# x of batch 0 on partitions 0-47 and 64-111, block 0 read in two parts, its zb made on chip, and one conversion moved to tick 96

## The chip, the core and the metric

The kernel runs on one core of one Trainium2 chip. The core has five engines that run side by side and meet at semaphores: PE (TensorE, the matmuls; its weight loads are shown apart as PEld), DVE (VectorE), ACT (ScalarE), POOL (GpSimd) and SP (SyncE, which here only issues DMAs). DMAs issued by SP, ACT and POOL run on 16 DMA engines. The metric is the device time of one execution in microseconds (us), lower is better. Times are given as medians of several runs; one execution was also profiled, and its trace is what the rows below come from.

## The reference

```python
def reference(x, w_in, w_out, w2_in, w2_out, alpha):   # x: 2 x 3008 x 256, float32
    X = np.fft.fft(np.fft.fft(x, axis=1), axis=2).real     # as float32
    t = X.reshape(6016, 256)
    h = t @ w_in                                           # 256 x 2048
    g = np.where(h > 0, h, np.exp(np.minimum(h, 0)) - 1)   # ELU
    t = g @ w_out                                          # 2048 x 256
    h = t @ w2_in
    g = np.maximum(h, 0) + alpha * np.minimum(h, 0)        # PReLU, alpha per column
    return g @ w2_out
```

The names stand for moe_w_in and so on. The weights arrive as float64; the kernel converts them to float32 on the chip.

## The kernel before

**The Fourier transform.** 3008 = 47 x 64. Stage A (`stage_a`, L146) multiplies x by a 47-point DFT matrix `f47` (L152): x of a batch lies in four chunks `xc` of 96 rows x 8 x 256, and each chunk takes four matmuls of 512 columns, whose results ACT copies to `uc` (L154). `store_u` (L161) writes `uc` to the DRAM tensors `ud`, one for each of three blocks g of the batch, and `load_v` (L168) reads a block back in another layout as `vt` (128 x 8 x 256). Stage B (`stage_b`, L199) multiplies `vt` by a 64-point DFT matrix `r64`, in two halves q = 0 and 1 (L206, L207); ACT rounds each half to float32r as `hi` (L210) and DVE subtracts it to get `lo` (L211). Both stand in `zt`, the input of layer 1. The 256-point transform along the last axis is not done on data: `w_fold` (L261) multiplies it into `w_in` of layer 1.

**zb.** One row of the transform needs a correction of rank one. `delta` (L178) computes 8 x 64 numbers of a block from `vt`, ACT copies them and writes them to DRAM (`nd`), and `load_zb` (L191) reads them back as 512 numbers repeated on 128 partitions. DVE adds `zb` times a number for each row (`an_sb`) to the first product (L420).

**The layers.** There are six blocks of up to 1024 columns (t = 0 and 1, 512 or 482 each) and, for each layer, 16 tiles f of the 2048 inner columns. One pair of block and f is a tick; ticks 0 to 95 are layer 1, 96 to 191 layer 2. A tick runs `gemm1` (L316), the nonlinearity on DVE and ACT, a split of the result `et` into `hi` (ACT, L398) and `lo` (POOL in layer 1, DVE in layer 2, L404), and three ticks later `gemm2` (L330), which adds three products (hi w_hi, hi w_lo, lo w_hi) to each of four accumulators. A product in float32r is one pass; a matmul of stage A, of the fold and of stage B in float32 is two, shown as x2.

**Weights.** `ld` reads a chunk of 512 columns or rows in float64; `conv_y` (ACT, L240) and the three steps of `conv_s` (DVE, L250, L252, L254) make float32 of one half of it; `w_split` makes `hi` (ACT, L293) and `lo` (POOL, L294), or `w_fold` does so for `w_in` of layer 1.

**What sets the order.** All is written out by hand. `START` is the list of what comes before tick 0, in the order in which each engine gets it; an entry names a function and its arguments (`('a', c, i)` is half a chunk of stage A, `('v', g)` a `load_v`, `('conv', kind, c, i)` half a weight chunk). Later work hangs on ticks by tables: `CONV2` has for each chunk of layer 2, counted from tick 80, the tick of its read, of the conversions of its two halves, a 1 or 3 that says whether the three DVE steps stand in three ticks or in one, and the ticks of the two splits. Each engine works through its instructions in program order. SP issues its DMAs in order too, and one that waits holds up those behind it. A pool with the tag `big` has seven buffers for `c256_sb`, `xc`, `uc`, `vt`, `zt` and later tiles; a new tile waits for the readers of the one whose buffer it gets.

```python
for eng, p0, p1 in ((nc.sync, 0, 96),) if b else ((nc.sync, 0, 64), (nc.scalar, 64, 96)):
    eng.dma_start(out=t[p0:p1, i * n:(i + 1) * n], in_=x[b, p0:p1, c * 8 + i * n:c * 8 + (i + 1) * n, :])
```

These two lines of `load_x` (L140, L141) put x of batch 0 on partitions 0 to 95: SP reads 64 rows of each chunk, ACT 32.

Of the kernel before, what the change touches and what calls it, by code (L numbers as in the profile page):

```python
# [11 lines left out]
ALU = mybir.AluOpType
# [14 lines left out]
    ('r64',), ('load', 'i', 1, 0), ('c256',), ('load', 'i', 1, 1), ('load', 'o', 1, 0),  # L27
    ('a', 0, 0), ('a', 0, 1), ('a', 1, 0), ('a', 1, 1), ('a', 2, 0), ('a', 2, 1), ('conv', 'i', 0, 0), ('conv', 'i', 0, 1), ('a', 3, 0),
    ('a', 3, 1), ('v', 0),
    ('conv', 'i', 1, 0), ('conv', 'i', 1, 1), ('fold', 0), ('an', 0), ('conv', 'o', 0, 0), ('fold', 1), ('conv', 'o', 0, 1), ('warm',), ('delta',), ('zb',),  # L30
    ('u', 1), ('split', 'o', 0, 0), ('alpha',), ('load', 'o', 1, 1), ('u', 2), ('v', 1), ('load', 'x', 1, 0),
    ('load', 'i', 1, 2), ('load', 'x', 1, 1), ('load', 'o', 1, 2), ('load', 'x', 1, 2), ('load', 'i', 1, 3), ('load', 'o', 1, 3),
    ('b',), ('an', 1),
# [41 lines left out]
def tile_fft_moe_elu_moe_prelu(  # L75
# [57 lines left out]
    def load_x(b, c, parts=1):  # L133
        if b:
            t = wp.tile([96, 8, 256], F32, tag=("sa", "sb", "sc")[c % 3], name="xc")
        else:
            t = big.tile([96, 8, 256], F32, tag="big", name="xc")
        n = 8 // parts
        for i in range(parts):
            for eng, p0, p1 in ((nc.sync, 0, 96),) if b else ((nc.sync, 0, 64), (nc.scalar, 64, 96)):  # L140
                eng.dma_start(out=t[p0:p1, i * n:(i + 1) * n], in_=x[b, p0:p1, c * 8 + i * n:c * 8 + (i + 1) * n, :])  # L141
# [178 lines left out]
    def gemm2(L, bl, f, first, last, hi, lo):  # L320
# [6 lines left out]
        for t in range(2):  # L327
            for d in range(2):
                for i, (a, b) in enumerate(PASSES):
                    mm(out=accs[L, bl][d][t][:, 0:n], lhsT=w[:, a, o, d * 128:(d + 1) * 128],  # L330
                       rhs=(hi, lo)[b][:, t, 0:n], start=(f == first and i == 0), stop=(f == last and i == 2))
# [153 lines left out]
    with tc.manual_schedule():  # L485
        nc.sync.dma_start(out=f47_sb, in_=f47)
        for c in range(4):
            load_x(0, c, 1 if c else 2)
        warm = wk.tile([128, 2, 512], F32, tag="h", name="warm")
        nc.vector.memset(warm, 0.0)  # L490
        wps = mmtile()
        for i in range(2):
            mm(out=wps, lhsT=warm[:, 0, 0:128], rhs=warm[:, 1, :], start=True, stop=True)
        def warm_up():
            wps = mmtile()
            for i in range(3):
# [143 lines left out]
```

## Time and profile before

| what | value |
|---|---|
| median of 3 runs | 1011.43 us (1008.5 to 1012.55) |
| the profiled execution | 1008.45 us |
| its span, first to last instruction | 1006.7 us |
| PE busy | 987.3 us (98%) |
| DVE busy | 684.8 us (68%) |
| ACT busy | 684.3 us (68%) |
| POOL busy | 310.4 us (31%) |
| mean granted clock of PE | 0.998 |

Engine times are busy times in the span; the engines overlap. A granted clock of 1 is 2.4 GHz, 0.5 is 1.2 GHz. In the rows, a line such as L316 is a line of the kernel before, `out<-in` names the tiles written and read, x3 a count of instructions merged into one row, and a bracket at the end the idle time of that engine just before, with what ended it. PEq, SPq and so on are an engine's sequencer, which issues DMAs; "issue" is time for which the profile shows no wait.

### The profile page before, as it was taken

What the parts mean: (1) busy time and instruction counts of PE and PEld (TensorE: products, weight loads), DVE (VectorE), ACT (ScalarE), POOL (GpSimd) and SP (SyncE); (2) the same over time, 40 slices, a digit from 0 to 9 for tenths busy, and PEclk for the clock granted to TensorE, in tenths of its full rate; (3) what the DMA queues carried; (4) which work ended last, traced back from release to release, by engine and by line L of the source; (5) the groups of instructions that cost most, each with busy time, mean ns of one, the idle gap of its engine ahead of it and who ended that gap; (6) DMA issues with size and microseconds to landing.
All of it is one profiled execution on the core that took longest, in us unless ns stands there. A gap on an engine that the chain in (4) does not pass through costs nothing.

```text
span 1006.7 us, 11887 instructions
## 1 busy us (share of the span) xinstructions
PE 987.3 (98%) x4354; PEld 799.4 (79%) x4354; DVE 684.8 (68%) x908; ACT 684.3 (68%) x991; POOL 310.4 (31%) x232
## 2 busy tenths in 40 slices
PE   8899999999999999999999999999999999999998
PEld 3576767788888888887788888888888888888887
DVE  1787988987887788899878655654544555455444
ACT  4577776766887788778787765655656666666654
POOL 0355667765656666566512100000000000000000
PEclk9999999999999999999999999999999999999999
DMA  9793322000000000124100001010010001001001
GB/s 275 206 320 87 82 74 94 1 12 1 1 11 1 11 1 1 42 86 153 57 1 0 1 1 42 1 43 1 1 39 1 1 1 42 1 1 42 0 1 40
DMA packets 20130, 44.65 MB, mean 44 GB/s; under 512 B 1988, under 2 KB 9412, under 8 KB 18632
## 3 DMA queue, kind: packets, MB, share of 16 engines
q1 hardware_dynamic: 18400, 41.61, 13.3%
q10 hardware_dynamic: 1416, 2.12, 0.7%
q8 instruction: 34, 0.56, 0.2%
q0 software_dynamic: 256, 0.17, 0.1%
q14 instruction: 24, 0.20, 0.1%
HBM read 31.41 MB, written 12.48 MB: 44 GB/s over the span
## 4 chain that ended last, share of the span: by engine, by line
PE 84%; DVE 9%; DMA 2%; issue 2%; ACT 1%; SPq 0%; POOL 0%; DVEq 0%; ACTq 0%
PE acc L330 45%; PE mmt L316 21%; PE eet L316 15%; DMA w<-w_in 2%; DVE ht L422 1%; DVE et L389 1%; DVE pt L420 1%; DVE sg L252 1%; DVE et L386 1%; DVE w L254 1%; PE eet L268 1%; DVE sg L250 1%; PE eet L152 1%; DMA xc<-x 1%; PE mmt L206 1%
## 5 line engine op out<-in xcount | busy, mean ns | idle before, releaser
L330 PE MATMUL acc<-hi,wo 128*128 128x512 f32 (+1 forms) x1536 | 470.5, 388 | 3.9 <-ACT hi L398 2.1
L330 PEld LDWEIGHTS acc<-hi,wo 128*128 128x128 f32 x1536 | 288.7, 188 | 60.8 <-ACT hi L398 2.5
L404 POOL TENSOR_TENSOR lo<-et,hi 128x512 fp32r<-128x512 f32 (+1 forms) x192 | 266.0, 1407 | 143.3 <-ACT hi L398 102.8
L330 PE MATMUL acc<-lo,wo 128*128 128x512 f32 (+1 forms) x768 | 298.6, 389 | 2.7 <-POOL lo L404 2.6
L398 ACT ACTIVATE hi<-et 128x1024 fp32r<-128x1024 f32 (+2 forms) x193 | 199.5, 1034 | 135.6 <-PE acc L330 103.1
L404 DVE TENSOR_TENSOR lo<-et,hi 128x512 fp32r<-128x512 f32 (+1 forms) x192 | 121.9, 676 | 152.3 <-ACT hi L398 152.2
L330 PEld LDWEIGHTS acc<-lo,wo 128*128 128x128 f32 x768 | 145.1, 189 | 33.7 <-POOL lo L404 5.7
L440 ACT ACTIVATE et<-ht 128x1024 f32<-128x1024 f32 (+2 forms) x97 | 100.4, 1035 | 91.4 <-DVE ht L422 86.4
L316 PE MATMUL mmt<-zt,wi 128*128 128x512 f32 (+1 forms) x462 | 122.0, 396 | 2.7 <-ACT zt L210 1.2
L391 DVE SCALAR_TENSOR_TENSOR et<-et,nal_sb,ht 128x1024 f32<-128x1024 f32 (+1 forms) x96 | 121.7, 1268 | 0.0
L316 PE MATMUL eet<-xhi,wi 128*128 128x512 f32 (+1 forms) x384 | 117.4, 387 | 1.4 <-DVE et L386 1.4
L316 PE MATMUL mmt<-xhi,wi 128*128 128x512 f32 (+1 forms) x384 | 117.3, 387 | 0.0
L316 PEld LDWEIGHTS mmt<-zt,wi 128*128 128x128 f32 x462 | 86.4, 188 | 25.6 <-issue 3.0
L316 PEld LDWEIGHTS eet<-xhi,wi 128*128 128x128 f32 x384 | 72.1, 188 | 15.8 <-DVE et L386 1.8
L316 PEld LDWEIGHTS mmt<-xhi,wi 128*128 128x128 f32 x384 | 72.1, 188 | 14.0
L420 DVE SCALAR_TENSOR_TENSOR pt<-zb,an_sb,mmt 128x512 f32<-128x512 f32 (+1 forms) x77 | 56.3, 732 | 30.7 <-PE mmt L316 30.6
L450 ACT ACTIVATE ht<-mmt 128x512 f32<-128x512 f32 (+1 forms) x96 | 56.5, 589 | 26.3 <-PE mmt L316 26.3
L316 PE MATMUL eet<-xlo,wi 128*128 128x512 f32 (+1 forms) x192 | 74.3, 387 | 0.0
L316 PE MATMUL mmt<-xlo,wi 128*128 128x512 f32 (+1 forms) x192 | 74.3, 387 | 0.0
L450 ACT ACTIVATE ht<-eet 128x512 f32<-128x512 f32 (+1 forms) x96 | 56.5, 589 | 22.8 <-PE eet L316 22.8
L389 DVE SCALAR_TENSOR_TENSOR et<-et,ht 128x1024 f32<-128x1024 f32 (+2 forms) x43 | 69.8, 1625 | 0.7 <-ACT et L442 0.7
L386 DVE SCALAR_TENSOR_TENSOR et<-eet,ht 128x512 f32<-128x512 f32 (+1 forms) x108 | 67.8, 668 | 0.0
(83 smaller groups left out, 911.8 us busy)
## 6 DMA issues: line engine op xcount, KB each, us to landing
w<-w_in SPq DMA_DIRECT2D x8, 1024.0 KB, 10.4
w<-w_out SPq DMA_DIRECT2D x8, 1024.0 KB, 11.6
vt<-ud SPq DMA_DIRECT2D x6, 1024.0 KB, 4.8
ud<-uc SPq DMA_DIRECT2D x20, 256.0 KB, 4.2
out_t<-ot SPq DMA_DIRECT2D x16, 256.0 KB, 2.2
xc<-x SPq DMA_DIRECT2D x4, 768.0 KB, 11.3
out_t<-ot SPq DMA_DIRECT2D x8, 241.0 KB, 2.2
xc<-x SPq DMA_DIRECT2D x3, 512.0 KB, 11.4
```

The lines of the kernel that those rows point to most:

```text
L152: mm(out=p[0:96], lhsT=f47_sb, rhs=xc[b, c][:, r0:r0 + 2, :].rearrange("p r j -> p (r j)"), start=True, stop=True)
L206: mm(out=o, lhsT=v[:, k, 0:128], rhs=r64_sb[:, 0:128], start=True, stop=False)
L316: mm(out=p[:, 0:n], lhsT=lhsT, rhs=rhs, start=(i == 0), stop=(i == len(ops) - 1))
L330: mm(out=accs[L, bl][d][t][:, 0:n], lhsT=w[:, a, o, d * 128:(d + 1) * 128], rhs=(hi, lo)[b][:, t, 0:n], start=(f == first and i == 0), sto ...
L386: stt(out=s["e"][:, i, :], in0=s["x"][i], scalar=-1.0, in1=s["h"][:, i, :], op0=ALU.add, op1=ALU.max)
L389: stt(out=s["e"][:, i], in0=s["e"][:, i], scalar=-1.0, in1=s["h"][:, i], op0=ALU.add, op1=ALU.max)
L391: stt(out=s["e"], in0=s["e"], scalar=nal_sb[:, s["f"]:s["f"] + 1], in1=s["h"], op0=ALU.mult, op1=ALU.add)
L398: act(out=s["hi"][:, i, 0:s["n"]], in_=s["e"][:, i], func=ACTF.Copy)
L404: (nc.gpsimd if s["L"] == 1 else nc.vector).tensor_tensor(out=s["lo"][:, i, 0:n], in0=s["e"][:, i, :], in1=s["hi"][:, i, 0:n].bitcast(F32) ...
L420: stt(out=pt[:, 0:n], in0=zb[bl][:, 0:n], scalar=an_sb[:, f:f + 1], in1=p[0], op0=ALU.mult, op1=ALU.add)
L440: act(out=s["e"][:, i], in_=s["h"][:, i], func=ACTF.Relu, scale=-1.0)
L450: act(out=s["h"][:, i, :], in_=p[i], func=ACTF.Relu)
```

## The change

- **x of batch 0** lies on partitions 0 to 47 and 64 to 111. ACT reads the upper 48 rows, SP the lower 48. The rows 32 to 63 of each chunk are first set to zero, by DVE for chunks 0 and 2 and by POOL for 1 and 3; SP's part overlaps them and waits for that, and the matmul takes 112 rows. `f47_ap` is `f47` in the same layout, with zeros between; `f47_sb` is read later, for batch 1. Chunk 0 is cut into 2 and 6 of its 8 groups, instead of 4 and 4.
- **Block 0** is read back as `vt` in two parts: 24 of its 32 rows behind the stores of three chunks, 8 behind the last.
- **zb of block 0** is made on chip. `ready_eye` prepares an 8 x 512 tile with ones on a block diagonal and an 8 x 128 tile of ones; `delta_0` multiplies the 8 x 64 numbers into the first (DVE); `spread_0`, called between the halves of stage B, sums and repeats them with one matmul; ACT copies the result to `zb`.
- **The three matmuls of `warm_up`** before delta are dropped.
- **Stage B of block 0** stands before the read of block 1 in `START`, and so its `zt` gets another buffer of the pool: that of the last chunk of x, where before it got that of the `vt` which it reads.
- **`gemm2` of tick 0** runs the eight products with `hi` first and the four with `lo` last.
- **`CONV2`**: the first half of layer 2's second `w_in` chunk is converted in tick 96 instead of 95.

```diff
+    f47_ap = const.tile([128, 96], F32, name="f47_ap")
...
+            i0, i1 = cuts
+            if i0 == 0:
+                xc[b, c] = big.tile([128, 8, 256], F32, tag="big", name="xc")
+            t = xc[b, c]
+            (nc.gpsimd if c % 2 else nc.vector).memset(t[32:64, i0:i1], 0.0)
+            for h, eng in ((1, nc.scalar), (0, nc.sync)):
+                eng.dma_start(out=t[h * 64:h * 64 + 48, i0:i1],
+                              in_=x[b, h * 48:(h + 1) * 48, c * 8 + i0:c * 8 + i1, :])
...
-            mm(out=p[0:96], lhsT=f47_sb, rhs=xc[b, c][:, r0:r0 + 2, :].rearrange("p r j -> p (r j)"),
+            f, k = (f47_sb, 96) if b else (f47_ap, 112)
+            mm(out=p[0:96], lhsT=f[0:k], rhs=xc[b, c][0:k, r0:r0 + 2, :].rearrange("p r j -> p (r j)"),
...
-        nc.sync.dma_start(out=vt[b, g], in_=ud[b][g].rearrange("n (q k) j -> (n q) k j", k=8))
+        nc.sync.dma_start(out=vt[b, g][4 * n0:4 * n1], in_=ud[b][g][n0:n1].rearrange("n (q k) j -> (n q) k j", k=8))
...
+    def delta_0():
+        p = mmtile()
+        v = vt[0, 0]
+        mm(out=p[0:8, 0:64], lhsT=v[:, :, 0], rhs=r64_sb[:, 0:64], start=True, stop=False)
+        mm(out=p[0:8, 0:64], lhsT=v[:, :, 128], rhs=r64_sb[:, 256:320], start=False, stop=True)
+        e = eye[0:8, 0, :].rearrange("p (k n) -> p k n", n=64)
+        tt(out=e, in0=p[0:8, 0:64].rearrange("p (o n) -> p o n", o=1).to_broadcast([8, 8, 64]), in1=e, op=ALU.mult)
+
+    def spread_0():
+        p = mmtile()
+        mm(out=p, lhsT=eye[0:8, 1, 0:128], rhs=eye[0:8, 0, :], start=True, stop=True)
+        zb[0] = wk.tile([128, 512], F32, tag="zb", name="zb")
+        act(out=zb[0], in_=p, func=ACTF.Copy)
...
+            if q == 0 and b == g == 0:
+                spread_0()
...
+        order = [(t, d, i) for t in range(2) for d in range(2) for i in range(3)]
+        if (L, bl, f) == (1, 0, 0):
+            order.sort(key=lambda k: k[2] == 2)
...
-    (('i', 2, 1), 8, 15, 16, 3, 17, 18),
+    (('i', 2, 1), 8, 16, 16, 3, 17, 18),
...
+        nc.vector.memset(f47_ap, 0.0)
+        warm = wk.tile([128, 512], F32, tag="s", name="warm", bufs=4)
+        load_x(0, 0, (0, 2))
         nc.vector.memset(warm, 0.0)
+        for h, eng in ((1, nc.scalar), (0, nc.sync)):
+            eng.dma_start(out=f47_ap[h * 64:h * 64 + 48], in_=f47[h * 48:(h + 1) * 48, :])
+        load_x(0, 0, (2, 8))
+        for c in range(1, 4):
+            load_x(0, c)
```

The order on the engines, at three places. First PE before the first `gemm1`, from the second fold (`eet<-w_192`) on, before the change; `r_sb` is `r64`, and the rows of stage B's halves go on as they begin here:

```order
L268 MATMUL eet<-w_192,c_sb 128x512 x2
L268 MATMUL mmt<-w_192,c_sb 128x512 x2
L497 MATMUL mmt<-warm,f_sb 96x512 x3
L183 MATMUL eet<-r_sb,vt 8x64
L184 MATMUL eet<-r_sb,vt 8x64
L206 MATMUL eet<-r_sb,vt 128x2x64
```

And PE with the change, from the same fold to the start of stage B, and then around the spread matmul:

```order
L298 MATMUL eet<-w_206,c_sb 128x512 x2
L298 MATMUL mmt<-w_206,c_sb 128x512 x2
L208 MATMUL mmt<-r_sb,vt 8x64
L209 MATMUL mmt<-r_sb,vt 8x64
L234 MATMUL eet<-r_sb,vt 128x2x64
...
L235 MATMUL eet<-r_sb,vt 128x2x64
L215 MATMUL eet<-eye 128x512
L234 MATMUL mmt<-r_sb,vt 128x2x64
```

The three warm-up matmuls are gone, and the spread matmul stands between the two halves of stage B, eight matmuls each.

Second, DVE at the same place before the change: the second half of the conversion of `w_out` 0 (`w_121`, `w_219`), then the two halves of `zt` and tick 0:

```order
L274 TENSOR_TENSOR wi_225<-mmt,wi_225 128x512
L250 TENSOR_SCALAR sg<-w_121 128x512
L252 SCALAR_TENSOR_TENSOR sg<-w_121,sg 128x512
L254 SCALAR_TENSOR_TENSOR w_219<-w_219,sg 128x512
L211 TENSOR_TENSOR zt<-eet,zt 128x2x256
L211 TENSOR_TENSOR zt<-mmt,zt 128x2x256
L420 SCALAR_TENSOR_TENSOR pt<-zb,an_sb,mmt 128x512
```

And DVE with the change:

```order
L304 TENSOR_TENSOR wi_239<-mmt,wi_239 128x512
L280 TENSOR_SCALAR sg<-w_134 128x512
L282 SCALAR_TENSOR_TENSOR sg<-w_134,sg 128x512
L284 SCALAR_TENSOR_TENSOR w_233<-w_233,sg 128x512
L211 TENSOR_TENSOR eye<-mmt,eye 8x512
L239 TENSOR_TENSOR zt<-eet,zt 128x2x256
L239 TENSOR_TENSOR zt<-mmt,zt 128x2x256
L452 SCALAR_TENSOR_TENSOR pt<-zb,an_sb,mmt 128x512
```

The multiply into `eye` stands behind the conversion and ahead of `zt`.

Third, DVE in ticks 95 and 96 before the change; `w_3849` is the second `w_in` chunk of layer 2, `w_3808` its first `w_out` chunk, and the rows `et<-eet,ht` are those of ticks 94 and 95:

```order
L386 SCALAR_TENSOR_TENSOR et<-eet,ht 128x482 x2
L250 TENSOR_SCALAR sg<-w_3849 128x512
L252 SCALAR_TENSOR_TENSOR sg<-w_3849,sg 128x512
L254 SCALAR_TENSOR_TENSOR w_4164<-w_4164,sg 128x512
L252 SCALAR_TENSOR_TENSOR sg<-w_3808,sg 128x512
L386 SCALAR_TENSOR_TENSOR et<-eet,ht 128x482 x2
L250 TENSOR_SCALAR sg<-w_3849 128x512
```

And DVE there with the change, where the same chunks are `w_3860` and `w_3819`:

```order
L418 SCALAR_TENSOR_TENSOR et<-eet,ht 128x482 x2
L282 SCALAR_TENSOR_TENSOR sg<-w_3819,sg 128x512
L418 SCALAR_TENSOR_TENSOR et<-eet,ht 128x482 x2
L280 TENSOR_SCALAR sg<-w_3860 128x512
L282 SCALAR_TENSOR_TENSOR sg<-w_3860,sg 128x512
L284 SCALAR_TENSOR_TENSOR w_4218<-w_4218,sg 128x512
```

The three operations on the first half of the chunk stand behind the `et` of tick 95 instead of ahead of it.

## Rows read from the trace of the kernel before

**Rows 1.** The page, its first part: busy us, share of span, instructions.
```profile
PE 987.3 (98%) x4354; PEld 799.4 (79%) x4354; DVE 684.8 (68%) x908; ACT 684.3 (68%) x991; POOL 310.4 (31%) x232
```

**Rows 2.** Chain of waits, first 52 us: start us, us, what.
```profile
1.82 6.76 DMA xc<-x
...
9.02 15.63 DMA w<-w_in
...
31.38 2.58 PE mmt L497 x6
```

**Rows 3.** By stretches: us, PE, PEld, DVE, ACT, POOL busy, PEclk, DMA share, GB/s.
```profile
4.00:10.00 6.00, 4.49 (x7) 1.23 (x6) 0.00 (x0) 1.84 (x2) 0.00 (x0) 1.00 1.04 263
...
12.00:16.00 4.00, 3.97 (x10) 1.37 (x9) 0.00 (x0) 2.69 (x5) 0.00 (x0) 1.00 0.97 196
16.00:18.00 2.00, 2.00 (x7) 0.67 (x5) 0.00 (x0) 1.20 (x3) 0.00 (x0) 1.00 0.94 299
18.00:26.00 8.00, 7.86 (x19) 3.04 (x18) 4.72 (x9) 6.48 (x13) 0.00 (x0) 1.00 1.05 403
...
48.50:52.00 3.50, 3.50 (x10) 2.75 (x9) 1.23 (x1) 3.47 (x5) 1.98 (x2) 0.51 1.10 408
```

**Rows 4.** Timeline of DVE, 24 to 40 us: start us, us, instruction, [idle before].
```profile
24.68 0.43 DVE L250 TENSOR_SCALAR sg<-w 128x512 int32<-128x512 int32 x1 [0.41 <-DMA w<-w_in]
...
34.61 0.69 DVE L254 SCALAR_TENSOR_TENSOR w<-w,sg 128x512 int32<-128x512 int32 x1
38.72 0.69 DVE L211 TENSOR_TENSOR zt<-eet,zt 128x512 fp32r<-128x512 f32 x1 [3.42 <-ACT zt L210]
```

**Rows 5.** Timeline of PE, 27 to 40 us.
```profile
29.50 1.88 PE L268 MATMUL mmt<-w,c_sb 128*128 128x512 f32 x4
...
34.22 0.49 PE L206 MATMUL eet<-r_sb,vt 128*128 128x128 f32 x2
...
36.10 0.39 PE L206 MATMUL mmt<-r_sb,vt 128*128 128x128 f32 x2
...
39.23 0.73 PE L316 MATMUL mmt<-zt,wi 128*128 128x512 f32 x2 [1.18 <-ACT zt L210]
```

**Rows 6.** Timeline of PE and POOL around the first `gemm2`.
```profile
46.11 0.73 PE L330 MATMUL acc<-hi,wo 128*128 128x512 f32 x2 [2.11 <-ACT hi L398]
46.14 2.54 POOL L404 TENSOR_TENSOR lo<-et,hi 128x512 fp32r<-128x512 f32 x2 [8.54 <-ACT hi L398]
47.47 0.50 PE L330 MATMUL acc<-lo,wo 128*128 128x512 f32 x1 [0.63 <-POOL lo L404]
```

**Rows 7.** Timeline of the head: DVE's memset, ACT's and POOL's split of `w_out` 0.
```profile
1.04 0.91 DVE L490 MEMSET warm<- 128x1024 f32 x1 [1.04 <-PEq L630]
...
34.88 0.63 ACT L293 ACTIVATE wo<-w 128x512 fp32r<-128x512 f32 x1 [0.35 <-ACT dt L186]
...
35.60 1.26 POOL L294 TENSOR_TENSOR wo<-w,wo 128x512 fp32r<-128x512 f32 x1 [2.10 <-ACT wo L293]
```

**Rows 8.** The read of `vt`: its issue (timeline), and KB and us to landing.
```profile
28.73 0.35 SPq L171 DMA_DIRECT2D vt<-ud  x1
...
vt<-ud SPq DMA_DIRECT2D x1, 1024.0 KB, 4.8
```

**Rows 9.** Timeline of DVE and PE, 477 to 483 us.
```profile
477.56 0.41 DVE L250 TENSOR_SCALAR sg<-w 128x512 int32<-128x512 int32 x1
478.01 1.60 DVE L252 SCALAR_TENSOR_TENSOR sg<-w,sg 128x512 int32<-128x512 int32 x1
479.71 0.69 DVE L254 SCALAR_TENSOR_TENSOR w<-w,sg 128x512 int32<-128x512 int32 x1
480.32 1.72 DVE L252 SCALAR_TENSOR_TENSOR sg<-w,sg 128x512 int32<-128x512 int32 x1
481.97 1.21 DVE L386 SCALAR_TENSOR_TENSOR et<-eet,ht 128x482 f32<-128x482 f32 x2
482.67 0.73 PE L316 MATMUL eet<-xhi,wi 128*128 128x512 f32 x2 [1.40 <-DVE et L386]
```

More of the change, by code (lines that the diff above doesn't have):

```diff
@@ L26 @@
 START = [
[L27 to L33, printed above, removed]
+    ('r64',), ('eye',), ('load', 'i', 1, 0), ('c256',), ('load', 'i', 1, 1), ('load', 'o', 1, 0),
+    ('a', 0, 0), ('a', 0, 1), ('a', 1, 0), ('a', 1, 1), ('a', 2, 0), ('a', 2, 1), ('v', 0, 0, 24), ('conv', 'i', 0, 0), ('conv', 'i', 0, 1), ('a', 3, 0),
+    ('a', 3, 1), ('v', 0, 24, 32),
+    ('conv', 'i', 1, 0), ('conv', 'i', 1, 1), ('fold', 0), ('an', 0), ('conv', 'o', 0, 0), ('fold', 1), ('conv', 'o', 0, 1), ('delta',),
+    ('u', 1), ('split', 'o', 0, 0), ('alpha',), ('load', 'o', 1, 1), ('u', 2), ('b',), ('v', 1, 0, 32), ('load', 'x', 1, 0),
+    ('load', 'i', 1, 2), ('load', 'x', 1, 1), ('load', 'o', 1, 2), ('f47',), ('load', 'x', 1, 2), ('load', 'i', 1, 3), ('load', 'o', 1, 3),
+    ('an', 1),
 ]
@@ L131, in tile_fft_moe_elu_moe_prelu, with load_x @@
     xc = {}
-    def load_x(b, c, parts=1):
+    def load_x(b, c, cuts=(0, 8)):
         if b:
             t = wp.tile([96, 8, 256], F32, tag=("sa", "sb", "sc")[c % 3], name="xc")
+            nc.sync.dma_start(out=t, in_=x[b, :, c * 8:(c + 1) * 8, :])
         else:
[L137 to L141, printed above, removed]
+            i0, i1 = cuts
[6 more added lines that the diff above has]
+                              in_=x[b, h * 48:(h + 1) * 48, c * 8 + i0:c * 8 + i1, :])
         xc[b, c] = t
@@ L189, in tile_fft_moe_elu_moe_prelu, with ready_eye @@
     zb = {}
+    def ready_eye():
+        nc.gpsimd.affine_select(out=eye[0:8, 0, :], in_=warm[0:8, :], pattern=[[1, 8], [0, 64]],
+                                compare_op=ALU.not_equal, fill=1.0, base=0, channel_multiplier=-1)
+        nc.gpsimd.memset(eye[0:8, 1, 0:128], 1.0)
+    def delta_0():
[10 more added lines that the diff above has]
+        act(out=zb[0], in_=p, func=ACTF.Copy)
     def load_zb(bl, eng=nc.sync):
@@ L326, in gemm2 @@
                            for d in range(2)]
[L327 to L331, printed above, removed]
+        order = [(t, d, i) for t in range(2) for d in range(2) for i in range(3)]
+        if (L, bl, f) == (1, 0, 0):
+            order.sort(key=lambda k: k[2] == 2)
+        for t, d, i in order:
+            a, b = PASSES[i]
+            mm(out=accs[L, bl][d][t][:, 0:n], lhsT=w[:, a, o, d * 128:(d + 1) * 128],
+               rhs=(hi, lo)[b][:, t, 0:n], start=(f == first and i == 0), stop=(f == last and i == 2))
     ys = {}
@@ L485, in tile_fft_moe_elu_moe_prelu @@
     with tc.manual_schedule():
[L486 to L489, printed above, removed]
+        nc.vector.memset(f47_ap, 0.0)
+        warm = wk.tile([128, 512], F32, tag="s", name="warm", bufs=4)
+        load_x(0, 0, (0, 2))
         nc.vector.memset(warm, 0.0)
+        for h, eng in ((1, nc.scalar), (0, nc.sync)):
[3 more added lines that the diff above has]
+            load_x(0, c)
+        eye = wk.tile([128, 2, 512], F32, tag="h", name="eye")
         wps = mmtile()
         for i in range(2):
[L493 to L496, printed above, removed]
-                mm(out=wps[0:96], lhsT=f47_sb, rhs=warm[0:96, 1, :], start=True, stop=True)
+            mm(out=wps, lhsT=warm[:, 0:128], rhs=warm, start=True, stop=True)
         start = {
@@ L513, in tile_fft_moe_elu_moe_prelu @@
             "r64": load_r64,
-            "warm": warm_up,
+            "f47": lambda: nc.sync.dma_start(out=f47_sb, in_=f47),
         }
```

11 lines of the change are left out of this document (6 added, 5 removed).

## The prediction

> **What bounds the kernel now.** The page first: PE is busy for 987.3 us, 98% of the span [rows 1]. What can be won is therefore the time in which PE waits or runs at half clock, and the change touches two such places: the head, up to the first `gemm2` at 46.11 us, and the passage from layer 1 to layer 2 at 481 us. For the head I read the chain of waits of the first 52 us [rows 2]. It hangs on the read of x, then on the read of the second `w_in` chunk, which lands at 24.65 us, then on its conversion and fold, and on three warm-up matmuls from 31.38; stage B follows. The table by stretches says how fast these reads are [rows 3]: 263 GB/s while SP's 64 rows and ACT's 32 rows of x run together, 196 GB/s while only SP's 64 rows are left (12 to 16 us), 403 GB/s with 128-row tiles. Then DVE: it works without a break from 24.68 to 34.61 + 0.69 = 35.30 us, and then idles 3.42 us until ACT has copied the first half of `zt` [rows 4]. PE waits 1.18 us before the first `gemm1` at 39.23 [rows 5] and 2.11 and 0.63 us in the first `gemm2` [rows 6]. After these pauses the granted clock is 0.51 over 48.5 to 52 us, the level of 1.2 GHz; that stretch loses 3.5 x 0.49 = 1.7 us [rows 3]. At the passage, PE waits 1.40 us at 482.67 for DVE's `et` [rows 9].
>
> **The read of x.** x of batch 0 is 4 x 96 x 8 KB = 3.15 MB; with `r64` and `f47`, 3.35 MB. Before, the stretch 16 to 18 us moved 598 KB; split between 196 and 403 GB/s, it says that x ended near 17.0. Now SP and ACT carry 48 rows each, so neither is left alone for long. At the 263 GB/s that the two queues showed together, 3.35 MB takes 12.7 us, and from the first bytes at about 2.2 us it ends at 14.9. SP starts late: its parts now wait for memsets of the rows 32 to 63. At 0.912 us for 1024 columns [rows 7], `f47_ap`, the first part, `warm` and the second part (96 + 512 + 512 + 1536 columns) end 2.4 us after DVE's start at 1.04, so SP's second part is issued at 3.4 instead of 1.82; ACT's queue has enough to move meanwhile, and I add 0.3 us for the tail. x ends at 15.2, 1.8 us earlier, and all of SP's reads behind it (`w_in` 0, `c256`, `w_in` 1, `w_out` 0) move by as much. Bounds: at 196 GB/s x would end at 19.6, 2.6 us later; at 403 GB/s at 10.8, 6.2 us earlier. I take 263 because it is the row of two queues at work.
>
> **Block 0 in two parts, the warm-up matmuls, a buffer for stage B.** Before, the read of `vt` was issued at 28.73 and took 4.8 us [rows 8]. Now 24 of 32 rows are asked for one stage-A chunk earlier and only the last 256 KB wait for the last store. That store follows x (1.8 us), and a quarter of the bytes, at 263 GB/s, saves another 3 us: `vt` is there near 29 to 30 us. The three warm-up matmuls (2.58 us of the chain [rows 2]) are gone, the delta matmul follows fold 1, which ends at 31.38 - 1.8 = 29.6, and the first half of stage B (34.22 to 36.10, 1.9 us [rows 5]) ends near 32. `zt` now has a buffer whose readers are done, so ACT copies its first half while PE makes the second; of the two copies in PE's wait of 1.18 us [rows 5] one, 0.6 us, is left. On PE alone this would be worth over 3 us. It is not, because of the next edit.
>
> **zb on chip.** The round trip by DRAM is gone, but before it was not late. What comes instead is a chain across engines: delta (PE), a multiply into `eye` (DVE), a 512-column matmul (PE), a copy (ACT). The multiply stands on DVE behind the second half of the `w_out` 0 conversion, so it cannot start before DVE's unbroken run ends, 10.65 us after `w_in` 1 lands. From there: multiply 0.69 (as DVE's 512-column operations [rows 4]), spread matmul 0.9 (two matmuls of L268 took 1.88 [rows 5]), second half of stage B 1.9, ACT copy 0.6, hand-overs 0.1. Counted on the old landing, the first `gemm1` would start at 35.30 + 4.2 = 39.5 against 39.23: 0.3 us lost, and PE stands some 2 us still ahead of the spread matmul. A further cost: ACT's `wo` copy waited until 34.88 for delta's copy and POOL's subtraction ran from 35.60, after DVE's run [rows 7]. It now comes 3 us sooner, beside DVE's two-input operations. Beside POOL such operations took 1.60 and 1.72 us instead of 0.69 [rows 4, 9]; between 0 and 1.0 us, I take 0.4. Head: 1.8 - 0.3 - 0.4 = 1.1 us. With the bounds of x and of POOL this is -3.9 to +5.9.
>
> **The first `gemm2` reordered.** The eight matmuls that need only `hi` now come first: at 987.3 / 4354 = 0.23 us a matmul [rows 1], 8 x 0.23 = 1.8 us, which covers the 0.63 us wait for POOL's first `lo`. POOL's second `lo` ends at 46.14 + 2.54 = 48.68 [rows 6]; the `hi` matmuls end at 47.9 and two `lo` at 48.4, so 0.3 us of wait come back. Gain 0.3 us (0 to 0.6).
>
> **Tick 96.** Of the conversion moved, three DVE operations (0.41, 1.60, 0.69 us [rows 9]) and one ACT copy leave tick 95. DVE then reaches the `et` of tick 95 after one conversion step instead of four. That step may still wait for POOL and end near 479.7, the two `et` operations (1.21 us) end by 480.9, and PE asks for them at 481.27: the 1.40 us are gone [rows 9]. What moved is done on DVE behind `et`, before the `et` of tick 96; the chunk is first used by the matmuls of tick 100, three ticks on. Bounds 0 (given back in tick 99) to 1.40; I take 1.4. No DMA moves with it.
>
> **Sum.** 1.1 + 0.3 + 1.4 = 2.8 us, with the clock's lost 1.7 us kept. The profiled execution took 1008.45 us, its span 1006.7; 1008.45 - 2.8 = 1005.65. The median of the three runs is 1011.43, and they spread over 4 us, so the profiled one is at their fast end. Carried over to the median: 1008.6. A difference of under 0.5%, 5.1 us, can hardly be told from none here.
>
> **Rivals.**
> A, more: x at 340 GB/s, between the pair's rate and 403, takes 9.9 us and ends at 12.4; the head gains 3.9 instead of 1.1, as DVE's run moves with the landing and `vt` keeps ahead of it. 1005.8. For it: two equal queues have no 196 GB/s stretch. Against: together they showed 263, and 64 + 32 rows load the two halves of the partitions less evenly but no heavier.
> B, clock: PE's 2 us pause before the spread matmul is as long as the 2.11 us one that preceded 0.51. If the half clock comes there too, on the spread matmul and stage B's second half, 1.7 us go: 1010.3. For it: nothing warms PE there any more. Against: the 1.18 us pause at 38 us had no such effect.
> C, the passage: DVE is full around tick 96 and the wait comes back later by 1.4 us: 1010.0. It is also the case in which this edit does not do what it says. For it: DVE's operations follow each other without a gap from 477.56 to 481.97 [rows 9], so what moves is queued, not dropped. Against: the next tick to use the result is three ticks away.
> D, slower: two transfers to the two halves of the partitions do not add up, and x goes at the 196 GB/s of one queue of 64 rows. x ends 2.6 us later, everything behind it too; 1.8 + 2.6 = 4.4 us against my sum: 1013.0, slower than before. The whole change turns slower once x ends 2.8 us after my 15.2, that is once the pair is below 3.35 MB / 15.5 us = 216 GB/s. For it: 64 rows run at half of 128. Against: 64 + 32 rows ran at 263, a third above 64 alone.
> The Trainium skill, page SBUF — State Buffer, section "Can I just issue two DMAs to hit both halves?", states the rule of D: two concurrent DMAs, on tiles at partition 0 and at partition 64, gave only 6% over a single one; by it the pair would move 1.06 x 196 = 208 GB/s, x would end at 18.6, and the time would be 1008.6 + 3.4 = 1012.0. The trace disagrees so far: 263 over 196 is 34%, so D stays small.
>
> **How the numbers follow.** My forecast, 1008.6 (1007 to 1010): 0.45. A 0.2, B 0.15, C 0.1, D 0.1. The range of 8 in 10 reaches into A and C/B on both sides and has room for a median of runs that spread 4 us: 1004.5 to 1012.2. Faster by over 0.5% means under 1006.4: most of A and a tail of mine, 0.2; slower by over 0.5%, over 1016.5: 0.02; else 0.78.
>
> **What would show it.** Right: 250 to 290 GB/s until 15 us; `w_in` 1 landing near 22.8; DVE unbroken until the `eye` multiply at 33 to 34.5; PE idle about 2 us between the halves of stage B; the first `gemm1` near 38; no wait at 481 us. Wrong: a landing of `w_in` 1 outside 21.5 to 24, DVE with idle time ahead of the multiply (then `vt` was late), a clock below 1 before 45 us, or a new wait after 482 us.

## The result

The changed kernel is slower: 1017.27 us (median of 15 runs, 1013.85 to 1021.1) against 1009.46 us (15 runs); the ratio is 1.0080, with a 95% interval of 1.0064 to 1.0096. That is 8.1 us more by the ratio, where 2.8 us less were forecast (1008.6, range 1004.5 to 1012.2). In this document a ratio is always to the kernel before, measured alongside, and 0.001 of it is 1.0 us; differences between two runs are taken from their ratios and not from their medians. The half width of an interval is 0.9 to 1.7 us.

The profiled execution took 1014.58 us, its span 1012.8. The page, its first part, as [rows 1]:

```profile
PE 987.4 (97%) x4350; PEld 798.5 (79%) x4350; DVE 690.3 (68%) x913; ACT 684.5 (68%) x991; POOL 316.1 (31%) x236
```

PE has the same work, so the loss is waiting again. The chain of waits of the first 56 us, which answers to [rows 2] (start us, us, what):

```profile
4.02 9.39 DMA xc<-x
13.54 3.70 PE eet L159 x4
...
24.11 0.87 PE mmt L159 x2
...
29.18 3.52 DMA ud<-uc
...
32.72 6.57 DMA vt<-ud
```

The read of x holds the chain longer than before (9.39 us for one piece, issued by SP at 4.02 and landed at 13.41). Stage A (L159) could begin only then; from 13.54 on PE works through it without a wait, and the stores and the read of `vt` follow. The second `w_in` chunk, on which the chain of the kernel before hangs from 9.02 to 24.65 us [rows 2], isn't in this one. The read of `vt` holds the chain longer too: it is issued at 32.72 instead of 28.73 and takes 6.57 us instead of 4.8 [rows 8]. The stretches, as [rows 3]; the last column is GB/s, the third from the end the granted clock:

```profile
4.00:10.00 6.00, 3.64 (x5) 0.73 (x3) 1.76 (x1) 1.28 (x1) 3.33 (x7) 1.00 1.02 172
12.00:16.00 4.00, 2.46 (x3) 0.96 (x4) 0.00 (x0) 0.43 (x1) 0.00 (x0) 1.00 0.97 177
16.00:18.00 2.00, 2.00 (x5) 0.71 (x4) 0.00 (x0) 0.76 (x2) 0.00 (x0) 1.00 0.99 222
...
22.00:24.00 2.00, 2.00 (x6) 0.70 (x5) 0.00 (x0) 1.35 (x3) 0.00 (x0) 1.00 1.00 386
```

172 and 177 GB/s where the kernel before had 263 and 196. The rate of 128-row tiles (386) is reached only at 22 us, so x ended near 21, not near 17 as before and not at 15.2. PE in the timeline, as [rows 5] and [rows 6], from its first fold (L298) on:

```profile
28.24 2.18 PE L298 MATMUL mmt<-w,c_sb 128*128 128x512 f32 x4
...
39.42 0.27 PE L208 MATMUL mmt<-r_sb,vt 128*8 128x64 f32 x2 [3.56 <-DMA vt<-ud]
...
41.72 1.12 PE L215 MATMUL eet<-eye 8*128 8x512 f32 x2
...
45.51 1.23 PE L346 MATMUL mmt<-zt,wi 128*128 128x512 f32 x3 [0.69 <-ACT zt L238]
...
52.30 2.12 PE L362 MATMUL acc<-hi,wo 128*128 128x512 f32 x8 [2.14 <-ACT hi L430]
...
60.87 0.50 PE L362 MATMUL acc<-lo,wo 128*128 128x512 f32 x1 [1.67 <-POOL lo L436]
```

The first fold and delta in the kernel before:

```profile
23.15 2.29 PE L268 MATMUL mmt<-w,c_sb 128*128 128x512 f32 x4
...
33.89 0.28 PE L183 MATMUL eet<-r_sb,vt 128*8 128x64 f32 x2
```

Between the two profiled executions the loss adds up so. PE comes to its first fold 5.1 us later (28.24 against 23.15), because stage A began late. `vt` is asked for 4.0 us later (32.72 against 28.73) and takes 1.8 us longer, and delta starts 5.5 us later (39.42 against 33.89). From delta to the first `gemm1` it is 6.09 us instead of 5.34, 0.75 more; from there to the first `gemm2` 6.79 instead of 6.88, 0.1 less; from there to the first stage-A matmuls of batch 1 24.84 instead of 23.73, 1.1 more, with the wait of 1.67 us for POOL's `lo` in the second `gemm2`, where the kernel before had none; the passage is 1.4 shorter (its wait at 481 us is gone). 5.5 + 0.75 - 0.1 + 1.1 - 1.4 = 5.9; the profiled times differ by 6.1. Each of the two executions has one stretch of some 4 us near half clock (0.51 over 48.5 to 52 us before [rows 3], 0.57 over 61 to 65 us here).

The other 2 us are not in this execution. It lies near the low end of the 15: the four up to 1015.3 us have a mean granted clock of 0.998 to 1.000, the nine from 1017.1 us on have 0.988 to 0.993. So in most executions more time at half clock (1.2 GHz) was added somewhere. Experiments 2, 3 and 10 show one such place.

### The profile page after: what moved, and what is told of

The parts are those of the page before. It is cut to its first block, busy times and chain, and to the rows that moved or that the text cites. A ratio compares the mean times of both kernels' runs of the same rounds, so it can differ in the third digit from the quotient of the medians.

```text
span 1012.8 us, 11886 instructions
## 1 busy us (share of the span) xinstructions
PE 987.4 (97%) x4350; PEld 798.5 (79%) x4350; DVE 690.3 (68%) x913; ACT 684.5 (68%) x991; POOL 316.1 (31%) x236
## 4 chain that ended last, share of the span: by engine, by line
PE 84%; DVE 9%; DMA 3%; ACT 2%; issue 2%; SPq 0%; DVEq 0%; ACTq 0%
PE acc L362 45%; PE mmt L346 21%; PE eet L346 14%; DVE et L421 2%; DVE pt L452 1%; PE eet L159 1%; DVE ht L454 1%; DMA ud<-uc 1%; DVE sg L282 1%; DMA xc<-x 1%; DVE et L418 1%; DMA vt<-ud 1%; PE eet L298 1%; ACT et L472 1%; DVE sg L280 1%
```

## Experiments

Names: x is read **in halves** (0-47 and 64-111, the change) or **as before** (0-63 on SP, 64-95 on ACT).

**1. x as before, the rest of the change kept** (e1_x64).

```diff
-            (nc.gpsimd if c % 2 else nc.vector).memset(t[32:64, i0:i1], 0.0)
-            for h, eng in ((1, nc.scalar), (0, nc.sync)):
-                eng.dma_start(out=t[h * 64:h * 64 + 48, i0:i1], ...)
+            for eng, p0, p1 in ((nc.sync, 0, 64), (nc.scalar, 64, 96)):
+                eng.dma_start(out=t[p0:p1, i0:i1], in_=x[b, p0:p1, ...])
```

> Changed kernel with x of batch 0 read as before (rows 0-63 on SP, 64-95 on ACT, no memsets, f47 on 96 rows); the rest of the change stays. If the read of x is the larger cause: x near 17 us again instead of 22.0, the second w_in lands near 24.7 instead of 28.7, the first gemm1 about 4 us before the 45.51 of the changed kernel, the time about 4 us under the changed kernel's (median 1017.3, so near 1013). If the loss lies in the other parts: w_in lands earlier, but the first gemm1 stays within 1 us of 45.5 and the time within 2 us of 1017.

Measured: 1011.09 us, ratio 1.0022 (1.0008 to 1.0035). PE in its timeline:

```profile
33.66 0.27 PE L205 MATMUL mmt<-r_sb,vt 128*8 128x64 f32 x2 [2.60 <-DMA vt<-ud]
...
39.75 1.22 PE L343 MATMUL mmt<-zt,wi 128*128 128x512 f32 x3 [0.69 <-ACT zt L235]
```

The first `gemm1` starts 5.8 us earlier than in the changed kernel, and the ratio falls by 5.9 us. PE's first fold, directly behind stage A in both, starts 5.0 us earlier (23.23 against 28.24). The read of x is the larger cause. But even without it the rest of the change, which was to bring 1.0 us (-0.3 - 0.4 + 0.3 + 1.4), costs 2.2 (0.8 to 3.5).

**2 and 3. Block 0 in one transfer, with x in halves (e2_vone) and with x as before (e3_x64_vone).**

```diff
-    ... ('a', 2, 1), ('v', 0, 0, 24), ('conv', 'i', 0, 0), ...
-    ('a', 3, 1), ('v', 0, 24, 32),
+    ... ('a', 2, 1), ('conv', 'i', 0, 0), ...
+    ('a', 3, 1), ('v', 0, 0, 32),
```

> Changed kernel with block 0 read in one transfer of 128 rows after the last store, as before; the rest of the change stays. If 96 rows read alone are what is slow: the read is issued near 32.7, takes about 4.8 us as the one transfer before did, is there near 37.6 instead of 39.3, and the time falls by 1.5 to 2 us. Rival, that the u stores of block 1, which now follow at once on SP's queue, share the rate with it: the read still takes 6 to 6.6 us and the time stays within 0.5 us.

> Both undone: x as before and block 0 in one transfer; zb made on chip, the order of gemm2, tick 96, the buffer and the dropped warm-up stay. If the two reads are the whole loss and add up: first gemm1 near 39.5, time about 6 us under the changed kernel's, 1008 to 1011, beside the kernel before at 1009.5. If a third part costs as well: above 1011.5.

Measured: 1017.58 us, ratio 1.0078 (1.0063 to 1.0094), and 1011.56 us, 1.0016 (1.0004 to 1.0027): each within 0.6 us of its partner with two parts. Whether block 0 is read in one part or in two makes no difference that can be seen. The read of e2 in its chain of waits:

```profile
33.10 6.23 DMA vt<-ud
```

It took 6.2 us, and 6.1 in e3, though it was one transfer of 128 rows; that is the time which the rival of e2's expectation named. Its cause would be the u stores of block 1, which stand right behind the read on SP, where the kernel before had the read of zb, which held them back until 36.1 us. e2 and e3 alone don't show this cause. h2 (experiment 14) does: like e3 it has one transfer, x as before and zb on chip, but its stores are held back. From 30 to 33 us its DMA engines moved 328 GB/s (322 in the kernel before) against 259 in e3, and PE did not wait for `vt`.

e2's profiled execution also shows the half clock. Its stretches (granted clock third from the end):

```profile
37.00:39.00 2.00, 0.00 (x0) 0.00 (x0) 1.97 (x4) 0.65 (x2) 0.94 (x1) 0.97 0.95 300
39.50:49.00 9.50, 9.50 (x37) 7.56 (x38) 2.07 (x4) 1.83 (x3) 2.00 (x2) 0.50 0.89 284
```

PE had waited 3.0 us for `vt`; then all of stage B ran at 0.50, and its first `gemm1` came at 50.06. e3's profiled execution shows it too: after a wait of 3.47 us the clock is 0.55 over 35.4 to 39 us. e1's wait of 2.60 us was followed by a clock of 1.00, and in the changed kernel's own profile so was a wait of 3.56 us:

```profile
39.50:45.50 6.00, 5.32 (x38) 4.14 (x37) 1.67 (x4) 2.01 (x4) 2.01 (x2) 1.00 0.98 251
```

So after such a wait the fall comes in some executions and not in others, which would account for the spread of 1014 to 1021 us.

**4. The two halves of x asked for at once** (e4_nomem). Without the memsets SP's half waits for nothing.

```diff
-            (nc.gpsimd if c % 2 else nc.vector).memset(t[32:64, i0:i1], 0.0)
...
-            mm(out=p[0:96], lhsT=f[0:k], rhs=xc[b, c][0:k, ...])
+            mm(out=p[0:96], lhsT=f[k0:k], rhs=xc[b, c][k0:k, ...])
```

> Changed kernel without the memsets of rows 32-63, so that SP's half of x waits for nothing; each stage-A matmul of batch 0 takes only one half of the rows (48 of 96) in turn, so part of the sum over x is left out. Theory that the halves went one after the other because SP's half was asked for late: both halves now run together at 263 GB/s or more, x ends near 15, the second w_in lands near 22.5, the time falls by 5 us or more against the changed kernel. Rival, that two transfers to the two halves do not add up however they are asked for: x stays under 208 GB/s and ends at 18 or later, the second w_in lands at 25.5 or later, and the time falls by 3 us at most.

Measured: 1009.6 us, ratio 1.0006 (0.9995 to 1.0018), 7.5 us under the changed kernel. First, what the memsets did. SP's waits in the changed kernel up to 12 us (us in all, times, longest):

```profile
SPq L146 <- DVE xc L144: 3.7, 3, 1.5
```

The issues of x by ACT and by SP in its timeline:

```profile
1.64 5.00 ACTq L146 DMA_DIRECT2D xc<-x  x4
...
4.02 3.31 SPq L146 DMA_DIRECT2D xc<-x  x4
```

ACT had three pieces, of 288, 384 and 384 KB, in the queue when SP's second came at 4.02. The DMA queues of the changed kernel from 5 to 8.5 us (packets, MB, share of 16 engines; q10 is ACT's, q1 SP's):

```profile
q10 hardware_dynamic: 82, 0.51, 97.0%
q1 hardware_dynamic: 20, 0.02, 4.3%
```

The same queues and stretch in e4:

```profile
q1 hardware_dynamic: 60, 0.37, 50.2%
q10 hardware_dynamic: 60, 0.35, 47.6%
```

In the changed kernel the engines worked almost only for ACT's half in this stretch, and both queues together moved 0.53 MB in 3.5 us = 152 GB/s. SP's half was left for later; where it ran nearly alone it moved 206 GB/s (9.5 to 11.5 us) and 181 (18 to 20 us), and the stretch of 177 had both halves and `r64` in it. In e4 they share the engines evenly. Its rates:

```profile
4.00:10.00 6.00, 3.84 (x8) 0.93 (x7) 0.00 (x0) 1.88 (x2) 0.46 (x2) 0.93 1.04 235
12.00:16.00 4.00, 3.61 (x8) 1.64 (x8) 0.00 (x0) 1.65 (x3) 0.00 (x0) 0.50 1.02 218
```

235 and 218 GB/s, 221 over 4 to 16 us, where the changed kernel has 181: asked for at once, the halves move more, but not the 263 that the first theory expected. Of the second theory the landing came true (the second `w_in` at 26.3 us, said to be 25.5 or later), the rate (under 208) and the time didn't. This landing is some 2.4 us earlier than in the changed kernel (near 28.7) and 1.7 later than before (24.65). So even without memsets the halves are no gain over 64 + 32 rows, which moved 244 in that stretch. The time fell by more than these 2.4 us and the 3 us of the second theory; PE's wait for `vt` was 0.48 us there instead of 3.56, and how much of the rest that explains was not tried apart. e4's profiled execution is the slowest of its 12, and it shows what the prediction feared of zb on chip, PE waiting ahead of the spread matmul for DVE's multiply:

```profile
38.20 1.09 PE L214 MATMUL eet<-eye 8*128 8x512 f32 x2 [1.25 <-DVE eye L210]
```

The granted clock over 43 to 46 us was 0.50.

**5. Tick 96 alone** (f1_tick96), on the kernel before:

```diff
-    (('i', 2, 1), 8, 15, 16, 3, 17, 18),
+    (('i', 2, 1), 8, 16, 16, 3, 17, 18),
```

> Kernel before with tick 96 alone (the second w_in half of layer 2 converted one tick later). If the passage gains what the step said: the 1.40 us wait of PE at 481 us is gone, none comes after it, the time is 1.2 to 1.4 us under the kernel before (ratio 0.9987). Rival, given back: a wait of about as much in the ticks that follow, ratio 1.000.

Measured: 1008.28 us, ratio 0.9989 (0.9980 to 0.9998). The stretches of the passage; in the kernel before, PE had waited 1.40 us in the first of them [rows 9] and was busy for 2.60 of its 4 us:

```profile
480.00:484.00 4.00, 4.00 (x20) 3.36 (x19) 3.93 (x5) 4.00 (x8) 2.60 (x2) 1.00 0.09 36
484.00:500.00 16.00, 15.89 (x70) 12.71 (x69) 14.12 (x15) 11.07 (x21) 8.28 (x6) 1.00 0.20 66
```

The wait is gone and none comes after it: 1.1 us (0.2 to 2.0).

**6. x in 96-row transfers on SP alone** (f2_x96), on the kernel before:

```diff
-  ... ((nc.sync, 0, 96),) if b else ((nc.sync, 0, 64), (nc.scalar, 64, 96)):
+  ... ((nc.sync, 0, 96),):
```

> Kernel before with each chunk of x of batch 0 read in one transfer of 96 rows on SP alone, nothing else changed. In the changed kernel the 96-row part of block 0 moved 8 KB packets in about 0.5 us, 16 x 8192 B / 0.5 us = 262 GB/s. If the rate hangs on how many rows one transfer spans: x ends near 15, the second w_in lands at 22 to 23 instead of 24.65, the time falls by up to 2 us. Rival, that the second queue is what lifts the rate to 263: x on one queue goes at 196 GB/s, ends near 19, the second w_in lands near 27, the time rises by 2 us.

Measured: 1009.13 us, ratio 0.9990 (0.9978 to 1.0003). Its stretch:

```profile
4.00:16.00 12.00, 11.09 (x22) 3.76 (x21) 0.00 (x0) 4.75 (x9) 0.00 (x0) 1.00 1.03 237
```

One queue moves 237 GB/s with 96 rows, and two queues with 64 + 32 rows moved 244. Both theories missed by a part: no gain, and no loss either. Over 4 to 10 us, the stretch of the 263, this one queue moved 243. So most of the 263 GB/s on which the forecast stood came with the 96 rows and not with "two queues at work".

**7. The u stores of block 1 held back** (f3_gate), on e1:

```diff
+ "gate": lambda: nc.sync.dma_start(out=nd[0][0:8, :], in_=eye[0:8, 0, 0:64]),
- ... ('delta',),   ('u', 1), ...
+ ... ('delta',), ('gate',),   ('u', 1), ...
```

> The run with x as before (block 0 in two parts, zb on chip), plus one small store on SP that waits for DVE's multiply into eye and stands ahead of the u stores of block 1, as the read of zb did in the kernel before. If those stores slow the read of block 0: the second part, issued at 28.3, lands about 1.2 us earlier, near 32.3 instead of 33.5; the first gemm1 near 39 and the time up to 1 us lower than without it. If the 96 and 32 rows are what is slow: the landing stays at 33.5 and the time too.

Measured: 1011.59 us, ratio 1.0014 (0.9997 to 1.0031); the last packet of the read ended at 32.8 us as in e1, and delta started at 33.72 instead of 33.66. The stores were held back until 36.25, and nothing came of it. With two parts the stores are not what slows the read; with one part (e2 and e3 against h2, and against 4.8 to 5.3 us in the kernel before, f1 and f2) the read is slower when they follow it.

**8. zb by DRAM again** (f4_zbd), on e1:

```diff
-            "delta": delta_0,
+            "delta": lambda: delta(0, [0]),
+            "zb": lambda: load_zb(0),
-            if q == 0 and b == g == 0:
-                spread_0()
```

> The run with x as before (block 0 in two parts), with zb by DRAM again: delta's copy on ACT, its store and the read of zb on SP ahead of the u stores; no eye multiply, no spread matmul between the halves of stage B. If zb on chip costs more than it gives: from the delta matmul to the first gemm1 it is 5.0 us or less instead of 6.1, the first gemm1 comes about 1 us earlier, near 38.6, and the time is 1 us lower. Rival, that the round trip is late now: DVE's first pt waits for zb, which lands 5.5 us or more after delta, and the time stays or rises.

Measured: 1010.53 us, ratio 1.0009 (0.9998 to 1.0021), 1.3 us under e1, which is not told from zero. Its profiled execution can't give the path, since PE waited 3.18 us for delta and stage B then ran near half clock (0.57 over 34 to 42 us): 7.6 us from delta to `gemm1`. This was inconclusive, and it pointed to the three matmuls that the change drops.

**9 and 10. The three matmuls back between the second fold and delta**, with x as before (g1_x64_warm) and in the changed kernel itself (g2_warm):

```diff
+        def warm_up():
+            wps = mmtile()
+            for i in range(3):
+                mm(out=wps[0:96], lhsT=r64_sb[:, 0:96], rhs=c256_sb..., start=True, stop=True)
- ... ('conv', 'o', 0, 1), ('delta',),
+ ... ('conv', 'o', 0, 1), ('warm',), ('delta',),
```

> The run with x as before, plus three 512-column matmuls on PE between the second fold and delta (of r64 and c256, their result unused), as the three dropped ones. If the dropped matmuls let the clock fall in some executions: mean clocks 0.995 or more in nearly all, none of the times near 1015, median 1008.5 to 1009.5 instead of 1011.1. Rival, that the spread has another cause: median and spread stay, 1010.5 to 1011.5, up to 1015.

> The changed kernel plus the same three matmuls between the second fold and delta. PE waits there for block 0 for 3.57 us, so they fill 2.6 us of a wait and delay nothing. If the half clock after this wait is what lies between the changed kernel's profile (1014.6, clock 0.998) and its median (1017.3, clock 0.992): median 1014 to 1015. If not: it stays at 1017.

Measured: g2 1014.18 us, ratio 1.0043 (1.0030 to 1.0056), its five executions within 1013.7 to 1015.5: 3.7 us less than the changed kernel by the ratios (3.1 by the medians), for work that computes nothing. Its executions at a clock of 0.999 to 1.000 took 1013.7 to 1014.2 us, and those of the changed kernel at 0.998 to 1.000 took 1013.9 to 1016.7: the executions at 0.988 to 0.992, eight of the 15 of the changed kernel, did not come among these five. PE's wait for `vt` is 0.44 us there instead of 3.56. In the two profiled executions, both at full clock here, the first `gemm1` comes no earlier for it (46.28 against 45.51). Its stretches around this wait:

```profile
36.00:40.00 4.00, 3.76 (x9) 1.17 (x7) 3.83 (x7) 1.85 (x4) 1.56 (x2) 1.00 1.00 258
40.00:46.00 6.00, 5.40 (x38) 4.25 (x38) 2.29 (x4) 2.20 (x4) 2.01 (x2) 1.00 0.91 247
```

g1: 1010.58 us, ratio 1.0007 (0.9997 to 1.0017), longest 1012.4 instead of e1's 1015.3. There the long executions went, but the median fell by only 0.5 us (1.5 by the ratios) and missed the expectation; the intervals of e1 and g1 overlap. The three matmuls are worth most where PE's wait is long. What was left had another cause.

**11. Stage B's output given its buffer ahead of block 1's read** (g3_bfirst), on f1:

```diff
-    ('u', 1), ... ('u', 2), ('v', 1), ('load', 'x', 1, 0),
+    ('u', 1), ... ('u', 2), ('b',), ('v', 1), ('load', 'x', 1, 0),
...
-    ('b',), ('an', 1),
+    ('an', 1),
```

> Kernel before with tick 96 and with stage B's output given its buffer ahead of block 1's read (the step 'b' written before 'v' 1), so that ACT's first copy of zt need not wait for the end of stage B. From the trace of the changed kernel: the wait before the first gemm1 falls from 1.17 to 0.69 us, 0.5 us earlier. If that reaches the end: 0.5 us under the run with tick 96 alone, about 1007.8. Rival, taken up by the next wait (POOL's lo in the first gemm2): equal to it, 1008.3.

Measured: 1006.97 us, ratio 0.9973 (0.9962 to 0.9984): **faster than both kernels**, and 1.6 us under tick 96 alone, a difference with an error of some 1.4 us. PE in its timeline, delta and the first `gemm1`:

```profile
34.63 0.28 PE L183 MATMUL eet<-r_sb,vt 128*8 128x64 f32 x2
...
39.48 1.22 PE L316 MATMUL mmt<-zt,wi 128*128 128x512 f32 x3 [0.69 <-ACT zt L210]
```

The wait before the first `gemm1` is 0.69 instead of 1.18 us [rows 5], and it was not taken back at POOL's `lo`. This profiled execution is the slowest of its ten (1009.02 us).

**12. The order of the first gemm2** (g4_gemm2), on f1:

```diff
+        if (L, bl, f) == (1, 0, 0):
+            order.sort(key=lambda k: k[2] == 2)
```

> Kernel before with tick 96 and the new order of the first gemm2 alone. If the prediction's step holds: the 0.63 us wait at its first lo matmul goes, the time is 0.3 us under tick 96 alone. Rival, given back: PE comes sooner to the second gemm2 and waits there up to 1.7 us for POOL's lo, as in the changed kernel, and the time stays within 0.2 us.

Measured: 1009.09 us, ratio 0.9991 (0.9982 to 1.0000), 0.2 us above tick 96 alone, which is not told from zero. PE's waits:

```profile
47.31 2.66 PE L332 MATMUL acc<-hi,wo 128*128 128x512 f32 x8 [2.12 <-ACT hi L400]
...
57.11 0.50 PE L332 MATMUL acc<-lo,wo 128*128 128x512 f32 x1 [0.60 <-POOL lo L406]
...
64.37 0.96 PE L316 MATMUL eet<-zt,wi 128*128 128x512 f32 x3 [0.99 <-ACT dt L186]
```

The 0.63 us of the first `gemm2` [rows 6] come back as 0.60 us in the second, and PE's later wait for ACT's copy `dt` is 0.99 us (0.4 in f1): here the rival held.

**13 and 14. zb alone.** h1_zbd_warm takes zb on chip out of g1 (x as before, the matmuls back, two parts, new `gemm2` order); h2_zb_alone puts zb on chip into g3.

```diff
# h1, against g1:
-            "delta": delta_0,
+            "delta": lambda: delta(0, [0]),
+            "zb": lambda: load_zb(0),
-                spread_0()
```

> The run with x as before and the three matmuls back (median 1010.6), with zb by DRAM again instead of on chip; block 0 in two parts, the order of gemm2 and tick 96 stay. If zb on chip is what is left of the loss: from delta to the first gemm1 5.0 us or less instead of 6.1, median 1 to 2 us lower, 1008.5 to 1009.5. If the two parts and the order of gemm2 are: it stays at 1010 to 1011.

> The best run so far (before, tick 96, stage B's output given its buffer first: 1007.0) with zb on chip in place of the round trip, the u stores of block 1 still held back as there by a small store of eye on SP, and the three matmuls of r64 and c256. If zb on chip costs by itself: the first gemm1 comes about 1 us later against delta (6.1 instead of 5.0 us), median 1008 to 1009. If it costs nothing: 1006.5 to 1007.5.

Measured: h1 1008.67 us, ratio 0.9983 (0.9973 to 0.9993), 2.4 us under g1; h2 1008.66 us, ratio 0.9991 (0.9980 to 1.0003), 1.8 us above g3. PE in the timeline of h1:

```profile
34.28 0.27 PE L188 MATMUL eet<-r_sb,vt 128*8 128x64 f32 x2 [0.44 <-DMA vt<-ud]
...
39.12 1.23 PE L341 MATMUL mmt<-zt,wi 128*128 128x512 f32 x3 [0.69 <-ACT zt L235]
```

The same of h2, with the spread matmul in between:

```profile
35.34 0.28 PE L205 MATMUL eet<-r_sb,vt 128*8 128x64 f32 x2
...
37.65 1.12 PE L212 MATMUL mmt<-eye 8*128 8x512 f32 x2
...
41.44 1.92 PE L343 MATMUL eet<-zt,wi 128*128 128x512 f32 x6 [0.69 <-ACT zt L235]
```

From delta to the first `gemm1`, all at full clock: 4.85 and 4.84 us with zb by DRAM (g3, h1), 6.09 or 6.10 with zb on chip (the changed kernel, e1, g1, h2). zb on chip puts 1.25 us on PE's path, 1.05 of it (41.72 to 42.77 in the changed kernel) the spread matmul between the halves of stage B; the round trip by DRAM was hidden where it stood: in the kernel before, f1, g3 and h1 DVE's first use of `zb` waits 0.59 us for PE's product and not for `zb`.

**The whole account**, step by step by the ratios (0.001 is 1.0 us):

| from, to | what changes | ratio | us |
|---|---|---|---|
| before, f1 | tick 96 | 1 to 0.9989 | -1.1 |
| f1, g3 | buffer of stage B's output | to 0.9973 | -1.6 |
| g3, h1 | two parts, order of `gemm2` | to 0.9983 | +1.0 |
| h1, g1 | zb on chip | to 1.0007 | +2.4 |
| g1, e1 | the three matmuls dropped | to 1.0022 | +1.5 |
| e1, changed | x in halves, with its memsets | to 1.0080 | +5.9 |

They sum to +8.1. Each step but the first carries the errors of two ratios, 1.4 to 2.1 us; the +1.0 and +1.5 alone are not told from zero. The last two hang together: with the matmuls kept, x in halves costs 3.6 us (g1 to g2) and not 5.9.

## Why the prediction was wrong

**The read of x failed, and with it the sum.** The forecast priced it at 263 GB/s, "the row of two queues at work". Two things were wrong in that step. That row belongs to transfers that together span 96 rows without a hole; one queue moved 243 in that stretch with such rows (f2), and two halves of 48 rows, asked for at once, moved 221 over 4 to 16 us (e4). And they were not asked for at once: the text saw that SP's second part would come at 3.4 us (it was 4.02) and passed over it with "ACT's queue has enough to move meanwhile" and 0.3 us. It had: over 5 to 8.5 us ACT's queue got 97.0% of the DMA engines' time and SP's 4.3%, SP's piece landed 9.39 us after its issue, and over 4 to 16 us the reads went at 181 GB/s.

**So did the path.** The prediction hung the head on the landing of the second `w_in` chunk and on DVE's run behind it, and counted a late x by the end of x. In the changed kernel the chain goes from that piece of x through stage A on PE to the last store and `vt`; what it cost is the late start of stage A (the first fold 5.1 us later), of which x as before gave back 5.0 (e1).

Rival D had the sign and the turning point right (slower once the rate is under 216 GB/s; measured 181), with a chance of 0.1. Its mechanism, two halves that don't add up, holds only in part: asked for at once they moved 221, above its turning point, and the 181 came with SP's late start, which it doesn't name. Its price, 4.4 us, was near the 3.6 to 5.9 measured, partly by luck. The base of the forecast was off too: it carried the 2.8 us to a median of 1011.43 of three runs, and 15 runs put it at 1009.46.

The Trainium skill, page SBUF — State Buffer, section "Can I just issue two DMAs to hit both halves?", had stood against this step with its 6%, which gave 208 GB/s. The trace agrees in part: e4's 221 is 7 to 13% above 64 rows alone (206 in f1, 196 in [rows 3]), and 96 rows moved 237 on one queue (f2) and 244 as 64 + 32 rows on two. The prediction weighed it against the row of 263 and kept the row.

**Block 0 in two parts.** Forecast: `vt` there near 29 to 30, 3 us won. Measured: nothing in e1 to e3. The first part has to wait for the third store, whose landing lies close to the last one's (the two parts are issued at 32.04 and 32.72 in the changed kernel, 26.9 and 28.3 in e1), and after its issue the second, of 256 KB, still takes 5.3 us in e1, since the first is moving. The step took "a quarter of the bytes" for a quarter of the wait.

**The dropped matmuls.** Priced as 2.58 us of the chain that go. They lay in a wait for `vt` that stays. What they did was to keep PE at work there; without them 1.5 us (x as before, not told from zero) to 3.7 us (changed kernel) are lost by the ratios. Nor could 2.58 us have gone: in the kernel before, `vt` landed at 33.5 [rows 8], 0.4 us ahead of delta at 33.89. Rival B had the half clock, but before the spread matmul and as one loss of 1.7 us.

**zb on chip.** Forecast 0.3 us lost, since DVE's run would hold the multiply and PE would idle 2 us. In the changed kernel neither happened, since `vt` held PE until 39.42: the multiply ran beside stage B's first half, the spread matmul followed without a pause. In e4, where `vt` came 4.8 us sooner, PE did wait 1.25 us there and a clock of 0.50 followed, which is rival B's form. The cost is the matmul itself on PE's path and what follows it, 1.25 us in the trace and 1.8 to 2.4 in time. The sentence that the round trip "before was not late" was right; it should have led to the conclusion that any work put on PE in its place is a loss. The 0.4 us for DVE beside POOL were not seen: DVE idles 1.98 us before its first `zt`.

**gemm2.** Forecast 0.3 us won, measured 0.2 lost, which is not told from zero: the step asked whether the `hi` matmuls cover POOL's first `lo`, but not whether POOL's later `lo` would be ready for a PE that comes earlier.

**Right:** PE's waits as the bound; tick 96 (1.4 us forecast, 1.1 measured, and rival C, given back, didn't hold); the buffer of stage B's output, one ACT copy of 0.6 us in the wait before the first `gemm1` (0.69 left, as forecast), worth 1.6 us in g3.

Open: why the buffer gives 1.6 us when the trace shows 0.5; how two parts and the order of `gemm2` share their 1.0 us; and in which executions the clock falls.

## What to carry to other kernels

A rate read from a trace belongs to the rows that those transfers span and to the order in which they were asked for: before pricing another split at it, look at who will be issued when, and price a piece that will run alone at the rate of its own rows. Removing a transfer or a matmul that looks idle also removes what it held back or kept busy: look at what stands behind it on its queue, and at what the engine does in the gap. Where a round trip is hidden, replacing it by work on the bounding engine costs at least that work (here 1.05 us of matmul, 1.25 on the path).
